# A new order table for an unchanged set of operations: linear attention and a gated MLP on one core

## The chip, the cores and the metric

The kernel runs on one NeuronCore of one Trainium2 chip. The metric is the device time of one execution in microseconds (us). Five engines run in parallel: PE (TensorE, matmuls; PEld is its weight load), DVE (VectorE), ACT (ScalarE), POOL (GpSimd) and SP (SyncE, which issues the DMAs).

## The reference

A gated recurrence over 768 steps for 4 batches of 8 heads with head dimension 48, and behind it an MLP with a spatial gate (d_model 384, d_ff 1024). All inputs are float32.

```python
for t in range(S):                       # q, k, v, alpha: (4, 8, 768, 48)
    state = alpha[:, :, t, :, None] * state + einsum('bhd,bhe->bhde', k[:, :, t], v[:, :, t])
    y[:, :, t] = einsum('bhd,bhde->bhe', q[:, :, t], state)
x = y.transpose(0, 2, 1, 3).reshape(B, S, H * D)
h = maximum(x @ w_in, 0); u, v = h[..., :512], h[..., 512:]
v_n = (v - mean(v)) / sqrt(var(v) + 1e-6)
v_s = einsum('ts,bsd->btd', w_spatial, v_n) + b_spatial[None, :, None]
out = (u * v_s) @ w_out
```

## The kernel before

**Tiling.** The 768 steps of a batch are 6 chunks of 128, so there are 24 chunks. Chunks 0 to 7 are worked in four pairs (`pair`, two steps a partition, loads of 384 KB), chunks 8 to 23 one by one (`first`, loads of 192 KB). Behind a chunk's attention come its parts of the MLP (`second_v`, `second_u`, and per batch `second_s`, `second_o`).

**Names.** Each operation has a key, written here with points. For pair j: `lnp.j` (ACT, logarithm of alpha, L443), `cump.j.par` (PE, cumulative sum with the triangle matrices le_pair and lt_pair, L452), `einvp` and `eexpp` (ACT, two exponentials of it, L460 and L469), `ktp` (POOL or DVE, k times one, L474) and `qtp` (DVE, q times the other, L481), `vbp` (cast of v), `tr.k`/`tr.q` (PE transposes, L502) and `ev.k`/`ev.q` (their copies to SBUF), `sc` (PE scores, L574), `m` (DVE, mask, L585), `updq` (PE, state update), `z` (DVE), `S` and `sb` (POOL: state times decay, state cast), `ya.j` and `y.i` (PE, output inside the pair and from the state), `xs`, `xt`, `xe` (the output cast, transposed, copied to `xT`). `lnp.1` reads the load `ac.2`, since loads are named by the pair's first chunk. Single chunks have the same steps without the p (`ln`, `cum`, `kt`, `trk`, `upd`). Then `v.b.t` and `u.b.f.h` (PE, first MLP matmul and its relu), `bn`, `rs`, `vn` (normalization of v), `s.b.d.h` (PE, spatial matmul on vn, six matmuls in two parts), `g` (gate product), `o.b.t` (last matmul) and `st` (store). Weights are loaded as float32 into two `raw_w` buffers and cast (`cast.w_in.half.n`, `cast.w_sp`, `cast.w_out`); w_spatial is transposed (`wt`, `we`). The constants are `c_*` operations: `c_m2.0` and `c_m2.1` (masks of the pairs), `c_m4`, `c_id` (identity), `c_tri` (le_pair and lt_pair), `c_sbd`, `c_qt`, `c_kt`, `c_la` (memsets). `b_sp` is the load of the spatial bias by POOL's queue, `bb.0` and `bb.1` its spread by PE, `be.0` and `be.1` its copy.

**The order.** Nothing is scheduled at run time. The text `PLAN` is one word an operation: the letter of the engine (P PE, D DVE, A ACT, G POOL, S SP's issue of a DMA, Q its landing, which emits nothing) and the operation's number. `replay` (called at L1129) emits the operations in that order, so each engine, and SP's DMA queue, gets its instructions in the order of its words and works them strictly one after another. A word says too which engine does an operation that several could do (`ENGINES`). Numbers behind a colon are filler: at the next PSUM bank taken, that many columns of a float32 matmul on the tile `junk` (L188), two passes each, go in front.

```python
for word in plan.split():
    number, *junk = word[1:].split(":")
    op, eng = ops[int(number)], LETTERS[word[0]]
    assert eng in op.eng and not op.done and all(d.done for d in op.deps), op.key
    fill.extend(int(x) for x in junk)
    op.emit(eng)
```

The durations given to `Op` (such as 1.46 us for a pair's load, `LP`) were for the planner that wrote the table; at run time they do nothing.

Of the kernel before, what the change touches and what calls it, by code (L numbers as in the profile page):

```python
# [54 lines left out]
LETTERS = {"P": "PE", "D": "DVE", "A": "ACT", "G": "POOL", "S": "SP", "Q": "DMA"}  # L55

PLAN = """
D0 S49 Q50 D17 D13 S109 Q110 G47 Q48 D5 S53 Q54 G10 D7 S51 Q52 D2 D3 D11 G18 D15 D12 D1 S55 Q56 A57 G14 S111 Q112 G16
P58:512:512:192 P264 A59 P68 A60 S113 Q114 G9 A69 D62 A70 D6 P66:512:232 S115 Q116 D71 P262 A67 D4 P74 A117 D61 S178
Q179 D72 A263 P128:492 D75 A265 P118 D73 A129 P76 S19 Q20 P64 A130 G131 D65 A119 D77 S180 Q181 A120 G63 D132  # L60
P134:512:108 P86 G121 D122 A135 P78 D87 S182 Q183 P126 D88 P124 P89 D80 S184 Q185 A186 P136 D91 A79 A127 D90 G81 A137
G123 D83 A125 G82 P149:512:500 A133 S322 Q323 P146 D151 P92 A22 D150 P96 A93 P197 D23 A97 D21 P94 D147 P187 A198 P98
A95 S24 Q25 D148 G200 A188 P100:228 A189 G190 P203 S326 Q327 A199 P138 D191 A101 D201 G84 A99 P195 D102 G8 A204 P205
G85 P193 A139 P103 D140 S324 Q325 A202 D206 G141 D196 P152 A104 D143 G142 A194 P215 S29 Q30 D105 G192 P153 A330 P157
G144 P207 D154 A106 G145 D158 P155 P331 D209 A156 D216 P341 A208 P159 G28 A332 D217 P212 A160 G210 A26 D214 P172 G211
A342 D213 P161 A333 G27 A173 D335 P218 S33 Q34 A343 A162 S328 Q329 P219 D345 P170 G334 A220 S382 Q383 D163 P223 P349
P221 A224 S384 Q385 P164 G344 D350 A222 P339 D174 A171 P225 P337 A165 P168 D340 A226 P166 D107 A175 D338 P227 A167
D176 D108 A169 P230 D32 A228 D177 P238 A231 D31 P247 S386 Q387 D35 A239 P347 D232 A248 P250 P244 A249 P242 G36 D229
A348 P236 A252 D251 P362 A233 S37 Q38 G346 D245 P253 D246 A243 G336 P240 D364 A237 S424 Q425 P351 A390 D363 A255 S428
Q429 D235 P359 A254 D234 P391 A352 D353 S388 Q389 P274 D360 A393 A241 G354 P270 A392 D356 P275 D361 A395 G394 P266  # L70
D276 P267 G357 D396 P271 A40 G39 D268 P398 D272 P259 S426 Q427 G355 A400 P365 D399 A261 D260 P256 G358 P405 S430 Q431
D366 A432 P369 P278 G269 D370 S495 Q496 P367 P433 D258 A368 P371 G273 D257 P279 S41 Q42 D407 A372 P294 A434 G397 D406
P295 A435 S461 Q462 G277 A437 D280 P376 S463 Q464 G436 P408 D296 P282 D438 A409 G439 P401 A377 P290 D402 A503 S465
Q466 P410 P440 G403 D411 P283 D412 A441 G281 D442 P373 D284 G297 P291 A374 P420 D292 S499 Q500 G285 A46 P447 D421 P443
P504 S497 Q498 A469 G43 D378 P413 A45 G404 P470 A44 S592 Q593 D449 P286 A472 A505 D448 P416 S467 Q468 A471 P287 D444
A474 D417 P418 G445 S501 Q502 A507 D288 P306 G473 A414 D508 S594 Q595 A419 P450 D415 G293 A307 P422 A451 S596 Q597
P298 D475 A423 G506 D375 S663 Q664 P477 A299 P452 G476 P302 A479 D453 D478 G289 A600 P480 P510 A303 D481 P484 S626
Q627 G446 D454 A512 P601 D511 P318 D485 G482 A602 S598 Q599 A603 A379 D486 P513 G483 P314 A605 S665 Q666 D515 G604
A319 P487 A509 D606 S628 Q629 P455 A488 D514 P608 S705 Q706 A456 D315 P489 P516 A610 D609 P310 S632 Q633 G607 D490
A517 D457 A491 P615 A671 P518 S630 Q631 P492 D519 A520 D381 A458 P521 D311 A493 D617 P530 A522 S667 Q668 D616 P528  # L80
A494 P611 D380 P534 S707 Q708 A529 D460 A634 P532 D459 D612 A523 S743 Q744 P548 G613 A531 P672 D524 P635 G641 S777
Q778 A713 P540 D533 A535 P618 A525 S709 Q710 P560 A674 A637 A636 D527 P544 D526 S669 Q670 A673 G638 P714 A639 P561
A676 S711 Q712 D640 P549 G614 A619 D677 P541 A715 S779 Q780 G675 D550 A716 P545 A751 D542 P642 S781 Q782 G551 P620
D562 P552 A622 D621 A718 S749 Q750 P553 D546 G543 A643 D719 P645 P623 A644 S745 Q746 D554 G717 A785 D646 P649 A678
P679 S747 Q748 G647 D650 P721 A624 P556 G547 A723 D651 P557 A681 D722 G563 P652 D680 S783 Q784 P682 D558 A653 P686
G555 P728 D683 S877 Q878 P654 D687 P536 A656 G684 A655 P537 D688 A720 S873 Q874 G648 P786 D729 P752 A787 P564 S907
Q908 G685 D538 A754 A758 P724 P657 D730 A753 S875 Q876 G539 A789 P565 D725 A658 D790 S990 Q991 P731 G755 A756 D566
P689 A732 P568 D757 G788 A690 D659 P759 A569 P733 S879 Q880 G726 P691 P576 D734 A692 G559 D625 A735 A760 S909 Q910
P762 P736 A761 G567 D693 D577 S944 Q945 A881 P792 D763 P766 G727 A794 D793 P882 S1027 Q1028 P694 D768 A737 G791 A883
D767 P699 G764 S986 Q987 A884 A695 P795 G765 P769 A886 S950 Q951 D796 P588 A700 G885 A915 D887 S948 Q949 P584 A770  # L90
D797 A696 S946 Q947 P889 D585 P771 A738 P798 D772 P701 A773 D891 A589 D799 P774 A890 D888 S911 Q912 D739 P703 A775
D702 P800 P896 S578 Q579 A704 D801 P580 A660 D802 D898 S304 Q305 P813 A581 D897 S988 Q989 P892 A740 P803 D776 S1023
Q1024 A952 P811 A994 S913 Q914 D661 P697 A814 D742 A804 P916 D741 P572 D893 S300 Q301 A917 D662 A918 P809 D805 G919
A920 S992 Q993 P815 A698 D812 A806 P953 S312 Q313 P829 A955 A573 D808 S590 Q591 P821 D807 A954 S1025 Q1026 D921 P995
A810 P822 G956 A997 S1029 Q1030 A996 P817 A957 D823 G894 S1057 Q1058 P899 A999 P825 D816 G959 A900 P830 D1000 G824
A922 S582 Q583 P818 D958 D831 P826 G998 D819 P901 P923 P960 A903 D827 S1059 Q1060 A925 P837 D902 G828 D820 A962 P926
P838 S1063 Q1064 D961 A924 P904 A1031 D839 S1061 Q1062 G895 P930 D927 A905 P967 S570 Q571 G832 P1002 D931 A1001 P1032
P845 A1004 D968 G928 A1034 P846 A1033 D932 A1003 P833 G1035 D969 A1036 P834 D847 P963 G929 P933 D1037 P853 A934 D964
D835 A1065 G965 P1039 P1009 A854 G1038 P935 D1040 P849 A936 S855 Q856 D1011 G966 A1041 P1005 P1066 A850 P841 D1006
A1067 D1010 S851 Q852 P970 A1069 G1068 P842 A937 D1070 P857 A971 G1007 D843 P972 G1071 P1072 D858 P1046 A973 G1008  # L100
A974 P1012 D1074 A1073 S859 Q860 D1047 P1042 G844 P978 A1013 D1043 P1014 D1048 P1075 A979 G1044 P938 A1015 D1077 G1045
P975 D1076 A939 G836 P1049 A1016 D940 A976 P1078 G840 P1017 A1050 D906 A1079 P982 G848 A1018 D977 P1051 P1080 P980
A1081 A1082 D1053 P861 A983 D1052 D981 P1095 D1019 A862 P1083 A941 A1020 P984 D942 A1084 D1022 P1054 D943 D1085 P1093
A1055 P869 A1096 D1056 A1094 P1089 P865 D1021 A1086 D985 P1097 D1090 A866 P1109 D1087 S867 Q868 P1105 D1088 S308 Q309
P1106 P1091 D1107 P1101 A1092 D870 G1108 P1102 S871 Q872 P1098 D1103 S574 Q575 P1110 D1104 S316 Q317 P1113 D1099 S863
Q864 P1114 S320 Q321 P1121 G1100 D1115 S586 Q587 P1125 D1111 P1122 D1116 G1112 P1126 D1123 P1117 D1127 P1118 D1124
P1128 D1119 P1136 A1129 G1120 P1132 S1130 Q1131 D1137 P1148 S1138 Q1139 A1133 P1144 D1149 S1134 Q1135 P1140 S1150
Q1151 D1145 P1152 S1146 Q1147 A1141 A1153 S1142 Q1143 S1154 Q1155
"""


# [1048 lines left out]
```

## Time and profile before

| | |
|---|---|
| time, median of 3 runs | 142.56 us (142.46 to 143.35) |
| the profiled execution | 142.43 us, its span 140.6 us |
| PE busy | 135.3 us (96%), 1921 matmuls |
| DVE, ACT, POOL busy | 118.5 (84%), 108.1 (77%), 83.9 us (60%) |
| DMA | 28.64 MB, mean 204 GB/s |
| granted clock of TensorE | 0.997 |

The span is the time from the first to the last instruction of the profiled execution; the time around it is the difference of the two numbers. A busy PE contains filler and is counted with modelled ends, so whether it has work without a gap is read from the spacing of its matmuls. DVE, ACT and POOL are idle most at the very start and at the end.

### The profile page before, as it was taken

What the parts mean: (1) busy time and instruction counts of PE and PEld (TensorE: products, weight loads), DVE (VectorE), ACT (ScalarE), POOL (GpSimd) and SP (SyncE); (2) the same over time, 40 slices, a digit from 0 to 9 for tenths busy, and PEclk for the clock granted to TensorE, in tenths of its full rate; (3) what the DMA queues carried; (4) which work ended last, traced back from release to release, by engine and by line L of the source; (5) the groups of instructions that cost most, each with busy time, mean ns of one, the idle gap of its engine ahead of it and who ended that gap; (6) DMA issues with size and microseconds to landing.
All of it is one profiled execution on the core that took longest, in us unless ns stands there. A gap on an engine that the chain in (4) does not pass through costs nothing.

```text
span 140.6 us, 4974 instructions
## 1 busy us (share of the span) xinstructions
PE 135.3 (96%) x1921; PEld 84.1 (60%) x1921; DVE 118.5 (84%) x292; ACT 108.1 (77%) x279; POOL 83.9 (60%) x148
## 2 busy tenths in 40 slices
PE   7999999999999999999999999999999999999990
PEld 3357566574767656665665765656657666566560
DVE  7187799989999789899689999999899899987850
ACT  3487898899976678999989699989967978751021
POOL 6816458861469996970289999402788599002520
PEclk9999999999999999999999999999999999999998
DMA  4999997989999979989999998999999120005535
GB/s 101 320 324 328 338 254 245 295 286 315 267 226 161 306 145 215 203 175 210 188 199 190 188 200 171 199 200 220 257 222 225 71 107 7 0 23 212 215 146 192
DMA packets 89000, 28.64 MB, mean 204 GB/s; under 512 B 83728, under 2 KB 87440, under 8 KB 88976
## 3 DMA queue, kind: packets, MB, share of 16 engines
q1 hardware_dynamic: 88944, 28.32, 81.8%
q8 instruction: 15, 0.25, 0.7%
q14 instruction: 9, 0.07, 0.2%
q0 software_dynamic: 32, 0.00, 0.0%
HBM read 23.60 MB, written 4.72 MB: 201 GB/s over the span
## 4 chain that ended last, share of the span: by engine, by line
PE 59%; ACT 9%; DMA 9%; SPq 7%; POOL 5%; DVE 5%; issue 4%; ACTq 0%; POOLq 0%
PE bank L819 42%; SPq L432 7%; DMA raw_w<-in_moe_w_in_dram 5%; DMA ac<-in_alpha_dram 3%; PE bank L710 3%; PE bank L745 2%; PE bank L773 2%; PE bank L731 2%; PE bank L657 2%; PE bank L767 1%; POOL kt L681 1%; DMA out_dram<-raw_w 1%; PE bank L389 1%; POOL kt L474 1%; ACT vn L880 1%
## 5 line engine op out<-in xcount | busy, mean ns | idle before, releaser
L819 PE MATMUL bank<-w_spT,vn 128*128 128x384 bf16 x192 | 35.9, 326 | 0.0
L980 POOL TENSOR_TENSOR gT<-vsb,uT 128x384 bf16<-128x384 f32 x27 | 25.0, 939 | 12.5 <-DVE vsb L967 12.1
L819 PEld LDWEIGHTS <-vn 128*128 128x128 bf16 x192 | 17.3, 97 | 10.2
L681 POOL TENSOR_TENSOR kt<-kc,binv 128x384 bf16<-128x384 f32 x16 | 14.6, 917 | 11.9 <-ACT bc L676 7.3
L756 DVE TENSOR_TENSOR ptm<-bank,mask 128x512 bf16<-128x512 f32 x32 | 20.5, 680 | 0.7 <-PE bank L745 0.6
L819 PE MATMUL bank<-xT,w_in 128*128 128x384 bf16 x96 | 19.9, 326 | 0.0
L967 DVE TENSOR_TENSOR vsb<-bank,bsp_bc 128x384 f32<-128x384 f32 x31 | 16.6, 551 | 3.6 <-PE bank L819 3.0
L819 PE MATMUL bank<-w_in,xT 128*128 128x512 bf16 x72 | 18.8, 379 | 0.3 <-ACT xT L198 0.2
L819 PE MATMUL bank<-w_out_sb,gT 128*128 128x384 bf16 (+1 forms) x100 | 18.6, 320 | 0.0
L198 ACT COPY kqT<-bank 128x512 bf16<-128x512 bf16 x28 | 15.9, 598 | 2.2 <-PE bank L710 1.5
L335 POOL TENSOR_TENSOR state<-state,bc 128x192 f32<-128x192 f32 x20 | 10.1, 506 | 12.4 <-DVE mvs L896 5.5
L200 POOL CAST sbd<-state 64x192 bf16<-64x192 f32 x40 | 13.7, 341 | 2.1
L204 ACT ACTIVATE v_sb<-bank 128x512 bf16<-128x512 f32 x20 | 12.0, 602 | 2.4 <-PE bank L819 2.3
L884 DVE BATCH_NORM_STATS2 stats<-v_sb 128x6 f32<-128x512 bf16 x20 | 13.6, 682 | 0.0
L204 ACT ACTIVATE uT<-bank 128x384 bf16<-128x384 f32 x23 | 10.9, 492 | 2.2 <-PE bank L819 2.0
L819 PEld LDWEIGHTS <-w_in 128*128 128x128 bf16 x96 | 8.7, 97 | 5.9
L198 ACT COPY xT<-bank 128x192 bf16<-128x192 bf16 (+1 forms) x25 | 9.0, 377 | 4.1 <-PE bank L389 2.9
L819 PEld LDWEIGHTS <-gT 128*128 128x128 bf16 x100 | 8.8, 97 | 5.0
L188 PE MATMUL bank<-junk 128*128 128x512 f32 (+6 forms) x22 | 10.7, 613 | 1.1 <-DVE junk L1050 1.1
L585 DVE TENSOR_TENSOR ptm<-bank,mask 128x512 bf16<-128x512 f32 x16 | 10.3, 682 | 1.0 <-PE bank L574 1.0
L198 ACT CAST x_sb<-bank 128x384 bf16<-128x384 f32 x19 | 9.0, 494 | 2.3 <-PE bank L773 2.3
L916 DVE TENSOR_SCALAR vn<-v_sb,mvs,rstd 128x512 bf16<-128x512 bf16 x24 | 8.9, 404 | 1.5 <-ACT rstd L909 1.5
(129 smaller groups left out, 281.2 us busy)
## 6 DMA issues: line engine op xcount, KB each, us to landing
ac<-in_alpha_dram SPq DMA_DIRECT2D x16, 192.0 KB, 4.0
kc<-in_k_dram SPq DMA_DIRECT2D x16, 192.0 KB, 4.0
qc<-in_q_dram SPq DMA_DIRECT2D x16, 192.0 KB, 4.2
vc<-in_v_dram SPq DMA_DIRECT2D x16, 192.0 KB, 4.0
raw_w<-in_moe_w_spatial_dram SPq DMA_DIRECT2D x3, 768.0 KB, 5.5
out_dram<-raw_w SPq DMA_DIRECT2D x11, 192.0 KB, 2.9
out_dram<-o_sb SPq DMA_DIRECT2D x9, 192.0 KB, 1.9
ac<-in_alpha_dram SPq DMA_DIRECT2D x4, 384.0 KB, 4.6
```

Source lines behind the costliest of these rows:

```text
L188: nc.tensor.matmul(out=flat[:, 0:cols].rearrange("p (a b) -> p a b", a=4), lhsT=junk, rhs=junk[:, None, 0:n].to_broadcast([128, 4, n]), st ...
L198: nc.scalar.copy(out=out, in_=in_)
L200: ENG[eng].tensor_copy(out=out, in_=in_)
L204: nc.scalar.activation(out=out, in_=in_, func=AF.Relu)
L335: ENG[eng].tensor_tensor(out=st["state"], in0=st["state"], in1=st["bc"][:, :, None].to_broadcast([128, HP, D]), op=ALU.mult)
L585: nc.vector.tensor_tensor(out=st[f"ptm{par}"][:, s], in0=st[f"pt{s}{par}"], in1=mask2[:, par], op=ALU.mult)
L681: ENG[eng].tensor_mul(out=k_blocks(kt3)[:, :, :, 0:D], in0=quad(st["kc"]), in1=st["binv"])
L756: nc.vector.tensor_tensor(out=st["ptm"][:, s], in0=st[f"pt{s}"], in1=mask4, op=ALU.mult)
L819: return lambda ps: nc.tensor.matmul(out=out(ps), lhsT=lhsT(), rhs=rhs(), start=start, stop=stop)
L884: nc.vector.bn_stats(out=stats, in_=d["v_sb"][:, tt, :])
L967: nc.vector.tensor_tensor(out=hold["vs"], in0=ps[:, 0:TH], in1=bsp_bc[:, th, :], op=ALU.add)
L980: ENG[eng].tensor_tensor(out=bt[b]["gT"][:, dsl, cols], in0=hold["vs"], in1=bt[b]["uT"][:, dsl, cols], op=ALU.mult)
```

## The change

Only the text `PLAN` is replaced. The operations, their instructions and their data are the same; 300 operations are on PE and 111 DMAs on SP in both tables. What differs:

- **Engines.** 108 operations change engine: 41 from ACT to DVE and 40 from DVE to ACT, 7 from DVE to POOL (among them `ktp.0.0`, `ktp.0.1`) and 6 back, 8 from POOL to ACT and 6 back.
- **Loads.** SP's order was ac.0, ac.2, qc.0, kc.0, vc.0, kc.2, qc.2, vc.2, ac.4, w_in.1, kc.4, qc.4, vc.4, ...; it is ac.0, ac.2, kc.0, qc.0, kc.2, qc.2, vc.0, ac.4, w_in.1, vc.2, qc.4, kc.4, vc.4, .... Later alpha loads move forward: ac.10 from place 31 to 24, ac.18 from 63 to 55, ac.23 from 87 to 68 (counted from 0).
- **Start of POOL.** It was b_sp, c_m4, c_m2.1, c_tri, c_m2.0, c_id, ktp.1.1; it is c_m2.0, b_sp, c_m4, c_id, c_tri, ktp.0.0, c_m2.1, ktp.1.1.
- **Start of PE and ACT.** PE took cump.0.0, bb.1, cump.0.1, tr.q.0.0 first; it takes bb.1, cump.1.0, cump.0.1, cump.0.0, bb.0, cump.1.1, tr.q.0.1. ACT took lnp.0 and four exponentials before lnp.1; it takes lnp.1 and lnp.0 first. `be.0` and `be.1` go from ACT to DVE.
- **Filler.** 4312 columns in six places become 3616 in four: 1216 in front of bb.1, 1140 of tr.q.0.1, 512 of sc.0.0, 748 of ya.0.

The beginnings of the two tables:

```diff
 PLAN = """
-D0 S49 Q50 D17 D13 S109 Q110 G47 Q48 D5 S53 Q54 G10 D7 S51 Q52 D2 D3 D11 G18 D15 D12 D1 S55 Q56 A57 G14 S111 Q112 G16
-P58:512:512:192 P264 A59 P68 A60 S113 Q114 G9 A69 D62 A70 D6 P66:512:232 S115 Q116 D71 P262 A67 D4 P74 A117 D61 S178
-Q179 D72 A263 P128:492 D75 A265 P118 D73 A129 P76 S19 Q20 P64 A130 G131 D65 A119 D77 S180 Q181 A120 G63 D132
...
+D0 S49 Q50 D1 D13 S109 Q110 D15 S51 Q52 D17 G16 D12 S53 Q54 D4 D3 D2 G47 Q48 G10 S111 Q112 G9 S113 Q114 A117 G14 A57
+S55 Q56 P264:512:512:192 P118 D265 P68 D11 P58 S178 Q179 A69 P262 D6 A59 P128 D5 A60 G61 D263 S19 Q20 A70 D62 A119 G18
+D72 A129 S115 Q116 A120 P76:512:512:116 A130 P64 D122 P66 G131 D65 S182 Q183 A73 D77 D67 G71 D132 P86:512 S180 Q181
...
```

In them P58 is cump.0.0, P68 cump.0.1, P118 cump.1.0, P128 cump.1.1, P264 bb.1, P262 bb.0, G47 b_sp, G10 c_m4, G14 c_tri, G16 and G18 c_m2.0 and c_m2.1, G9 c_id, A57 lnp.0, A117 lnp.1, G61 and D61 ktp.0.0.

## What was predicted, before the result was known

> **What bounds the kernel now.** I read the busy time by stretches first, to see where an engine is full. Columns: stretch, its length, then busy us (and instructions) of PE, PEld, DVE, ACT, POOL, the granted clock, DMA share, GB/s.
>
> ```profile
> 0.00:20.00 20.00, 18.95 (x217) 10.47 (x217) 13.48 (x43) 13.98 (x28) 10.57 (x26) 1.00 1.00 278
> 20.00:40.00 20.00, 19.26 (x395) 12.99 (x394) 19.01 (x47) 18.50 (x50) 11.87 (x25) 1.00 0.99 281
> 40.00:120.00 80.00, 79.72 (x1206) 50.30 (x1205) 72.58 (x175) 69.17 (x187) 57.61 (x95) 1.00 0.86 184
> 120.00:140.60 20.60, 17.35 (x109) 10.33 (x107) 13.46 (x30) 6.40 (x18) 3.89 (x4) 0.98 0.37 134
> ```
>
> From 40 us on TensorE is never without work: 79.72 of 80. From 20 to 40 DVE (19.01) and ACT (18.50) are as full as PE. Only the first 20 us have slack, and there the PE time is partly filler (L188, junk).
>
> The chain that ended last says the same in order of time: a DMA queue and the first weight at the start, one row of 93 second-stage matmuls at the end.
>
> ```profile
> 9.02 1.22 SPq L432
> 10.29 6.88 DMA raw_w<-in_moe_w_in_dram
> ...
> 39.45 2.95 PE bank L819 x18
> ...
> 119.20 15.55 PE bank L819 x93
> ```
>
> 93 matmuls in 15.55 us are 167 ns each, a 384-column matmul without a gap. So the time is: when the dense part starts (first vn matmul at 39.3 us), plus 98 us to the last matmul at 137.3, plus an end of 3.3 us (last copy, store, landing) to 140.6. The profiled execution took 142.43, 1.8 more than its span; the median is 142.56.
>
> The start, instruction by instruction:
>
> ```profile
> 1.22 0.67 POOL L1104 DMA_DIRECT2D b_sp_sb<-in_moe_b_spatial_dram  x1 [0.78 <-POOLq L1144]
> 5.27 0.52 PE L452 MATMUL bank<-la,le_pair 128*128 128x384 bf16 x1
> 5.50 1.37 POOL L241 TENSOR_SCALAR_AFFINE_SELECT mask<-mask 64x512 bf16<-64x512 bf16 x2
> 7.18 0.55 DVE L481 TENSOR_TENSOR qt<-qc,bank 128x384 bf16<-128x384 f32 x1 [3.20 <-ACT bank L469]
> 19.51 0.82 PE L819 MATMUL bank<-w_in,xT 128*128 128x512 bf16 x3
> ```
>
> The bias load leaves early, the first cumulative sum runs at 5.27, the first qt product at 7.18 and the first v matmul at 19.51.
>
> **What the change can and cannot move.** The operations are the same; 108 of them change engine and nearly all change place. TensorE's real work is identical. I summed each PE operation's usual spacing: 112.5 us in both orders. In the 98 us of the dense part the irregular waits (over 0.15 us) add to 1.2 us, the largest 0.34 at 75.9 us for a kt of POOL; the rest is work and a regular 0.13 us where one shape follows another. So behind 40 us the new order can win at most 1.2 us and can lose more.
>
> **The supply of instructions** was the planner's aim. The page shows PE's reads as a queue of their own:
>
> ```profile
> q8 instruction: 15, 0.25, 0.7%
> ```
>
> Fifteen packets of 16 KB, 0.9 to 1.8 us each. The first began at 17.35 us with 357 PE instructions done, the second at 20.81 with 481; the trace shows no PE wait that ends with one. I cost this part at 0; what covers it is that a block arrives some 200 instructions early. Without that cover one late read would cost up to 1.8 us. The Trainium skill (Runtime: NRT & Kernel Launch, Instruction fetch mechanics) speaks against the aim too: it says an engine fetches blocks of 256 instructions ahead by itself and that crossing one is mostly hidden; 0.25 MB in 15 packets agrees with the block, and by that rule too the term is 0.
>
> **The start, walked by hand.** Durations are those of the rows; 0.05 to 0.2 us is added from engine to engine as the rows show it. Loads of 384 KB follow each other at 1.2 us (issue rows 1.15 to 1.22 apart), landing from 4.25 on; w_in's 768 KB took 3.2.
>
> 1. POOL now begins with one mask (1.37, cannot start before DVE's memsets, 1.9), then the bias load, mask4 (1.05), ident (0.57) and only then the triangles (1.2): le_pair and lt_pair end at 6.9 instead of 5.55. The bias issues at 3.3 instead of 1.22; its landing took 3.5, so 6.8. PE's first real operation is now the bias matmul, so all four cumulative sums queue behind it, and DVE's copy of the bias (be.1) stands ahead of sbd's, qt's and kt's memsets. First sum 7.1 instead of 5.27. Filler (1216 columns) ends at 5.27 as before; total filler falls from 4312 to 3616 columns, which lies in these waits.
> 2. ACT takes both logarithms first (ac of pair 1 lands at 5.5), so the eight exponentials run in a row from 7.95 to 11.3. Before they ended at 12.5, since lnp.1 stood behind them and the two bias copies were ACT's.
> 3. DVE's first qt product: 9.4 instead of 7.18. Both first kt move from DVE to POOL (0.91 for 0.55), which delays the second one to 13.0.
> 4. scores, masks, ya.0: 17.45 (17.22 before). The 748 filler columns ahead of it (1.3 us) fit the wait for the last mask.
> 5. vc of pair 1 is now behind w_in and lands at 17.2 instead of 12.8, w_in at 16.0 instead of 17.2. x_sb of chunk 0 comes at 18.2 (17.83), the first v matmul at 20.5 (19.51).
> 6. kc of pair 2 is moved behind its qc: 20.2 instead of 18.28. POOL's kt of pair 2 starts at 20.25 (19.22), and the states behind it on POOL give y.2 and y.3 at 24.6 to 24.9 (24.15 and 24.33).
> 7. From there the new order catches up: updq.2 is already done, w_in.0 lands at 26.1 in both, v.0.2 and v.0.3 end at 28.4 in both; the first four u end at 32.7 (32.3).
> 8. First vn matmul: 39.2 (39.3). The matmuls of sc.3.0 (about 0.3) are then still to do.
>
> Start: 39.2 + 0.3 - 39.3 = +0.2 us. Bounds: -0.7 if all PE idle from 20 to 40 (20 - 19.26) vanishes; +2.3 if step 3's lateness is never given back.
>
> **Behind 40 us.** Loads are further ahead: with landing times shifted by the new queue order, no k, q, v or alpha of chunk 10 or later lands less than 4.5 us before PE uses it (before: 3.2, ac of 10). Alpha of chunk 23 goes out 19 places earlier. I find the chains PE to engine to PE no tighter than before: the shortfalls of PE work against their minimum length add to under 0.5 us in both. DVE's share up to y.21 is 2 us larger, inside more than 10 us of slack there. Bounds: -1.2 (all waits gone) and +2.2 (half of the 4.4 us that PE loses beyond its spacing from 20 to 40, the nearest stretch that waits). Nothing excludes either; I take +0.3, near zero because the row says 79.72 of 80.
>
> **End.** Last copy on DVE (0.36) for ACT (0.32), same stores: 0.0, between -0.2 and +0.3.
>
> **Sum:** 0.2 + 0.3 + 0.0 = +0.5. Span 141.1; with 1.8 around it 142.9 against 142.43; on the median 143.1.
>
> **Rivals.**
> (a) Slower: step 3's lateness stays. DVE is 95% busy from 20 to 40; if its small waits stay as long as they were (3.4 us from 7.2 to 39.3), it starts 2.3 us late and its shorter list up to the last vn of batch 0 (27.2 us of work against 28.7, by the rows) gives nothing back, since the two kt that it sheds first go to a POOL that is itself late. Then the dense part starts 2.3 us late: 142.56 + 2.3 = 144.9. It decides from the point where DVE's first qt product comes after 10.5 us, when the landings at 17.2 and 20.2 no longer cover it. For it: DVE and ACT full; against: the waits at loads in steps 5 and 6.
> (b) The clock. Filler passes of 512 columns ran 0.85 us apart until 4.6 us and 0.43 from 7 on; the clock record starts full speed at 6.79. The new order leaves PE idle from 5.3 to 6.8. If full speed comes one such stretch later, ten 384-column matmuls take 0.34 instead of 0.162 (+1.8) and the 1140 filler columns 3.8 instead of 1.9; of these 3.7 about half hides behind steps 5 and 6: +1.9, 144.5. The Trainium skill (TensorE: Matmul & The Clock Gate, Part 1) says that the gate looks at free-running windows of about 3.4 us and opens after a busy one; the trace's 6.79 allows that.
> (c) Faster: start at its low bound (-0.7) and all 1.2 us of dense waits gone: 142.56 - 1.9 = 140.7. For it: earlier loads, 1.4 us less DVE work ahead of the first vn; against: 1.2 is all there is.
> (d) A late instruction read stops PE: +1.8, 144.4. Against: step above.
>
> **Chances.** Forecast 0.46, (a) 0.27, (b) 0.08, (c) 0.15, (d) 0.04. One per cent (1.4 us) is about what a measurement here tells from no change. Faster is (c), 0.15; slower (a), (b), (d), 0.39; same 0.46. The forecast's own range is 142.0 to 144.0. For 8 in 10 I reach to most of (c) and past (a) for start and dense losses together: 141.0 to 145.8.
>
> **What would show it.** First cumulative sum near 7.1 and bias landing near 6.8 (step 1); first qt 9.4; ya.0 17.5; first v matmul 20.5; y.3 near 24.6; first vn matmul near 39.2; PE busy over 79 of 80 from 40 to 120. Wrong if the first vn matmul is off by more than 1.5 us, or if 40 to 120 holds PE waits of over 2 us.

## The result, and the profile after

| | before | after |
|---|---|---|
| time, median of 6 executions each | 142.95 us (142.46 to 144.57) | 144.88 us (143.92 to 146.68) |
| the profiled execution, its span | 142.43, 140.6 us | 144.01, 142.2 us |
| start of the last matmul in the trace | 136.85 us | 138.45 us |

The new order is slower: after to before is 1.0116 [1.0073, 1.016]. In the profiled executions the last matmul starts 1.60 us later, and what follows it is as long as before. The executions differ in the granted clock: in three of the six the mean clock was 0.988 (spans 143.0 to 143.4), in two 1.0 (142.1 and 142.2). Ratios leave out executions over 1.5% above the fastest of the same kernel, here the one with a span of 144.9. The mean clock shows a fall back to half speed but not a late start of full speed: the profiled execution of experiment 3 has a mean of 1.000, although its record of full speed begins only at 13.45 us.

Busy time by stretches of the changed kernel (columns as before the change):

```profile
0.00:20.00 20.00, 17.59 (x249) 10.46 (x250) 13.44 (x43) 12.19 (x25) 13.03 (x30) 1.00 1.01 286
20.00:40.00 20.00, 18.29 (x338) 11.79 (x342) 18.83 (x43) 19.03 (x50) 12.25 (x23) 1.00 0.95 270
40.00:120.00 80.00, 78.30 (x1192) 50.16 (x1200) 73.08 (x176) 65.73 (x180) 56.89 (x92) 1.00 0.85 179
120.00:142.20 22.20, 18.89 (x135) 11.07 (x132) 14.97 (x35) 9.59 (x27) 1.06 (x1) 1.00 0.39 144
```

PE's share fell in both middle stretches, 19.26 to 18.29 and 79.72 to 78.30. Part of this fall is only in the record: the trace of after holds 59 of the 72 matmuls of v (`w_in<-xT`), 36 of 48 between 40 and 120 us, and a missing matmul looks like a hole. Experiment 2 below, which differs in the place of one cast and has a complete trace, shows

```profile
40.00:120.00 80.00, 79.43 (x1216) 50.24 (x1214) 72.85 (x175) 65.96 (x180) 56.76 (x92) 1.00 0.85 180
```

The largest holes of after that are not beside a missing matmul are 0.42 us before 104.66, 0.24 before 91.94 and 0.21 before 83.36. The chain of waits of after, in order of time:

```profile
11.90 7.56 DMA kc<-in_k_dram
19.60 0.93 POOL kt L474
...
32.24 1.11 DVE w_row L200
33.90 1.24 PE bank L819 x5
35.65 1.57 PE bank L819 x9
39.66 3.04 PE bank L819 x18
...
102.88 0.74 issue
104.66 2.11 PE bank L819 x12
...
121.23 16.41 PE bank L819 x98
```

A cast of w_spatial (w_row) now stands in front of the dense part, and the last row of second-stage matmuls starts later. That this chain begins with a load of k and a kt of POOL comes from a gap in the record: the first of the three matmuls of v.0.0 is missing, and the one at 20.56 is the second. Where all three are recorded (experiment 2, whose start is the same), the chain comes from the bias load and the exponentials:

```profile
3.23 3.49 DMA b_sp_sb<-in_moe_b_spatial_dram
...
9.63 0.79 ACT binvp L460 x2
...
18.66 0.49 ACT binvp L460
20.37 0.83 PE bank L819 x3
```

The page's instruction queue is unchanged:

```profile
q8 instruction: 15, 0.25, 0.7%
```

To see where the 1.60 us come from, I took each PE operation's start and compared the two orders at equal PE work done (the sum of the operations' usual spacings, 112.5 us in both). The table gives the delay against the trace of before, for the changed kernel and four experiments explained below; the first column is the time in the trace of before. Which spacing is called usual moves single entries by some tenths; the difference between two columns of the new order in one row, and the last row, are firmer.

| us in before | after | sb.18 early | start of POOL | no meetings | start only |
|---|---|---|---|---|---|
| 5.27 | +1.46 | +1.49 | +0.14 | +1.53 | +1.54 |
| 12.5 | +0.77 | +0.80 | +0.52 | +0.83 | +0.86 |
| 17.4 | +0.09 | +0.13 | -0.15 | +0.17 | +0.19 |
| 31.7 | +0.19 | +0.24 | +1.18 | +0.16 | +0.30 |
| 33.7 | +1.18 | +0.46 | +1.40 | +0.47 | +0.52 |
| 39.5 | +0.44 | -0.31 | +0.56 | +0.10 | +0.05 |
| 44.1 | +0.50 | -0.26 | +0.62 | +0.16 | +1.03 |
| 75.5 | +0.69 | +0.02 | +0.89 | +0.42 | +1.03 |
| 92.8 | +0.55 | -0.22 | +0.67 | +0.19 | +1.03 |
| 97.9 | +0.92 | +0.16 | +1.04 | +0.56 | +1.04 |
| 103.2 | +1.55 | +0.49 | +1.67 | +0.89 | +1.04 |
| 136.7 | +1.60 | +0.53 | +1.72 | +0.95 | +1.03 |

Three things stand in the column of after. The start is 1.46 us late and next to nothing of that is left at 17.4. A step comes at 33.7, partly given back. Another comes between 93 and 103 and stays. The start, from the timeline of the changed kernel:

```profile
3.23 0.67 POOL L1104 DMA_DIRECT2D b_sp_sb<-in_moe_b_spatial_dram  x1
5.32 1.58 ACT L443 ACTIVATE la<-ac 128x768 bf16<-128x768 f32 x2 [3.29 <-DMA ac<-in_alpha_dram]
6.72 0.32 PE L848 MATMUL bank<-b_sp_sb,ones_row 1*128 1x384 bf16 x1 [1.25 <-DMA b_sp_sb<-in_moe_b_spatial_dram]
6.97 0.34 PE L452 MATMUL bank<-la,le_pair 128*128 128x384 bf16 x1
9.25 0.56 DVE L481 TENSOR_TENSOR qt<-qc,bank 128x384 bf16<-128x384 f32 x1
```

The two later steps begin at DVE. Timeline of DVE, then of POOL, in the changed kernel:

```profile
32.16 1.17 DVE L200 CAST w_row<-raw_w 128x768 bf16<-128x768 f32 x1
34.85 1.16 DVE L916 TENSOR_SCALAR vn<-v_sb,mvs,rstd 128x512 bf16<-128x512 bf16 x2
...
102.55 1.14 DVE L200 CAST sbd<-state 64x192 bf16<-64x192 f32 x2
104.06 0.56 DVE L691 TENSOR_TENSOR qt<-qc,bank 128x384 bf16<-128x384 f32 x1
```

```profile
32.04 0.89 POOL L200 CAST w_row<-raw_w 128x768 bf16<-128x768 f32 x1
34.72 0.83 POOL L200 CAST w_row<-raw_w 128x768 bf16<-128x768 f32 x1
...
102.60 1.86 POOL L980 TENSOR_TENSOR gT<-vsb,uT 128x384 bf16<-128x384 f32 x2 [0.28 <-DVE vsb L967]
```

Each DVE row runs beside one of POOL that began just before it or, for the pair of casts of sb.18, just after its first. I call that a meeting. PE waits at the end of both, in the first and the last of these rows (bracket: idle time and what ended it; the row between them is a wait for a kt of POOL):

```profile
33.39 0.35 PE L831 MATMUL bank<-ident,w_row 64*128 64x64 bf16 x12 [0.70 <-DVE w_row L200]
91.94 0.29 PE L710 MATMUL bank<-ident,kt 64*128 64x64 bf16 x8 [0.24 <-POOL kt L681]
104.66 0.65 PE L819 MATMUL bank<-w_spT,vn 128*128 128x384 bf16 x3 [0.42 <-DVE qt L691]
```

### The profile page after: what moved, and what is told of

Read it like the earlier page. It is cut to its first block, busy times and chain, and to the rows that moved or that the text cites. A ratio compares the mean times of both kernels' runs of the same rounds, so it can differ in the third digit from the quotient of the medians.

```text
span 142.2 us, 4928 instructions
## 1 busy us (share of the span) xinstructions
PE 133.1 (94%) x1904; PEld 83.5 (59%) x1917; DVE 120.3 (85%) x294; ACT 106.5 (75%) x280; POOL 83.2 (59%) x145
## 4 chain that ended last, share of the span: by engine, by line
PE 51%; DVE 14%; POOL 8%; SPq 8%; issue 6%; DMA 5%; ACT 5%; DVEq 0%; POOLq 0%
PE bank L819 38%; SPq L432 7%; DMA kc<-in_k_dram 5%; POOL gT L980 3%; DVE stats L884 2%; PE bank L710 2%; POOL kt L681 2%; POOL sbd L200 2%; PE bank L773 1%; DVE vn L916 1%; PE bank L745 1%; DVE ptm L585 1%; PE bank L831 1%; PE bank L389 1%; ACT binv L669 1%
## 5 line engine op out<-in xcount | busy, mean ns | idle before, releaser
L819 PE MATMUL bank<-w_spT,vn 128*128 128x384 bf16 x192 | 35.3, 326 | 0.5 <-DVE qt L691 0.4
L980 POOL TENSOR_TENSOR gT<-vsb,uT 128x384 bf16<-128x384 f32 x25 | 22.8, 923 | 16.5 <-DVE vsb L967 16.4
L819 PEld LDWEIGHTS <-vn 128*128 128x128 bf16 x192 | 17.6, 97 | 11.3 <-issue 0.5
L819 PE MATMUL bank<-xT,w_in 128*128 128x384 bf16 x96 | 19.2, 326 | 0.0
L819 PE MATMUL bank<-w_in,xT 128*128 128x512 bf16 x59 | 16.0, 379 | 1.3 <-issue 0.3
L198 ACT COPY kqT<-bank 128x512 bf16<-128x512 bf16 x22 | 12.4, 592 | 6.0 <-PE bank L710 4.5
L200 POOL CAST sbd<-state 64x192 bf16<-64x192 f32 x36 | 12.3, 341 | 1.9
L198 ACT CAST x_sb<-bank 128x384 bf16<-128x384 f32 x21 | 9.8, 483 | 3.7 <-PE bank L773 2.7
L200 DVE COPY kqT<-bank 128x512 bf16<-128x512 bf16 x26 | 10.1, 414 | 0.5 <-PE bank L502 0.5
L188 PE MATMUL bank<-junk 128*128 128x512 f32 (+3 forms) x18 | 9.2, 647 | 1.1 <-DVE junk L1050 1.1
L916 DVE TENSOR_SCALAR vn<-v_sb,mvs,rstd 128x512 bf16<-128x512 bf16 x24 | 9.5, 431 | 0.7 <-ACT rstd L909 0.7
```

What stands on the lines that cost most here:

```text
L198: nc.scalar.copy(out=out, in_=in_)
L200: ENG[eng].tensor_copy(out=out, in_=in_)
L819: return lambda ps: nc.tensor.matmul(out=out(ps), lhsT=lhsT(), rhs=rhs(), start=start, stop=stop)
L916: nc.vector.tensor_scalar(out=d["vn"][:, t, :], in0=d["v_sb"][:, t, :], scalar1=d["mvs"][:, t, 0:1], scalar2=d["rstd"][:, t:t + 1], op0=AL ...
L980: ENG[eng].tensor_tensor(out=bt[b]["gT"][:, dsl, cols], in0=hold["vs"], in1=bt[b]["uT"][:, dsl, cols], op=ALU.mult)
```

## The experiments

Theory A: the new order puts DVE's casts and copies beside POOL's work, and each such meeting lengthens a DVE instruction that PE is waiting for. Theory B: the loss lies in the order otherwise, in its start or in waits spread over it, as each expectation says. Theory C: the hole in PE's work at 5.3 to 6.8 us upsets the clock.

**1. sb.18 back on POOL** (one word of the new order).

```diff
-P923 D895 G828
+P923 G895 G828
```

> sb.18 goes back from DVE to POOL, at the same place of the table; nothing else. Theory A (DVE and POOL block each other): in the changed kernel sb.18's two casts took 1.14 us on DVE (102.55 to 103.69) beside POOL's gate product, for 0.52 us of sb.1 when POOL was idle; qt.21 and with it the PSUM bank of s.2.0.0 came late, and PE stood 0.58 us. Without it DVE has 1.1 us less ahead of qt.21, the PE wait before s.2.0.0 goes, and the time falls by 0.6 to 0.9 us: ratio to before about 1.005 to 1.008, span about 141.4. Theory B (the late start of the first 10 us is carried to the end): no change, 1.011 to 1.012. Theory C (POOL's place is what counts: sb.18 then delays the gate products by 0.73 us): PE waits for kt.21 or a g instead, time within 0.3 us of the changed kernel.

Ratio 1.0145 [1.0094, 1.0196], no gain. In the trace the step between 98 and 103 us shrank from 0.63 to 0.05, so the wait was this cast's. But that execution lost 1.6 us elsewhere: its delay at 12.5 us was 2.36 instead of 0.77. The stretch from 6.8 to 11 us of this kernel shows why:

```profile
6.80:11.00 4.20, 4.03 (x12) 1.72 (x12) 3.35 (x10) 2.79 (x7) 1.44 (x2) 0.60 1.15 317
```

The granted clock there was 0.60, where before and after have 1.00. The clock record has full speed from 4.25, half speed from 7.66 to 11.07, then full speed again. PE did 12 matmuls where after did 24. What theory C describes is at work in this execution. Its price in the times isn't clear: the four executions with a mean clock of 0.988 or less had spans of 142.7 to 143.2, the two others 142.8 and 144.1.

**2. sb.18 early on DVE** (behind vn.2.4, where POOL is idle).

```diff
-A902 A920 D807 P825
+A902 A920 D807 D895 P825
...
-P923 D895 G828
+P923 G828
```

> sb.18 stays on DVE, but goes ahead of the relu u.2.3.1, at about 100.0 us, where POOL was idle from 95.3 to 100.5. DVE's list has the same length. Theory A: the two casts take about 0.5 us in place of 1.14, so 0.6 us of the 1.1 is gained: time falls by 0.4 to 0.7 us against the changed kernel, ratio about 1.007. If only sb.18's own work on DVE counts and not the meeting with POOL, the casts take 1.1 us there too or the time stays at 1.011. Theory B: 1.011.

Ratio 1.0109 [1.006, 1.0158], where A gave about 1.007 and B 1.011; the profiled execution came at a span of 141.2, 1.0 below after's, the others at 141.7 to 144.5. In that trace both meetings at which PE waited are gone:

```profile
32.02 0.55 DVE L200 CAST w_row<-raw_w 128x768 bf16<-128x768 f32 x1
...
99.23 0.52 DVE L200 CAST sbd<-state 64x192 bf16<-64x192 f32 x2
```

The casts took 0.52 and 0.55 instead of 1.14 and 1.17. For w_row nothing was changed: POOL was at another cast, which had begun 0.16 us ahead of DVE's, while a normalization of DVE still ran, and was itself the one that took longer (1.06 for 0.5). Which one loses changed with a few tenths of a microsecond. The table's column shows both gains: 0.72 at 33.7 and 0.3 behind 98.

**3. The other half of the first meeting: cast.w_sp.0.1 from POOL to ACT.**

```diff
-P230 G32 A245
+P230 A32 A245
```

> The cast of the second piece of w_spatial (cast.w_sp.0.1) goes from POOL to ACT, at the same place; DVE's list is unchanged. In the changed kernel DVE's cast.w_sp.0.0 took 1.17 us (32.16 to 33.33) while POOL worked on cast.w_sp.0.1 (32.04 to 32.92); before it took 0.55. PE stood 0.87 us in front of wt.0. Theory A: cast.w_sp.0.0 takes 0.55 us again and PE starts wt.0 near 32.8 in place of 33.39; the first vn matmul comes 0.2 to 0.5 us earlier (39.1 to 39.4 for 39.59), the end as much, unless ACT's 0.67 us more takes it back: ratio 1.008 to 1.011. If DVE's order alone made the cast late, it stays at 1.17 us and nothing moves. Theory B: nothing at the end.

Ratio 1.0162 [1.0119, 1.0205], a miss. DVE's cast took 0.55 and the step at 33.7 shrank to 0.2, as A wants, but the time did not follow, and sb.18 met POOL again (1.14). In the profiled execution full speed began only at 13.45 us, so its span of 146.4 says nothing on the order. The other five lie at 143.3 and 143.4, three of them with a mean clock of 0.988 and two with 1.0: here the dip left no mark on the span. Whether this kernel is slower than after is not shown, since the intervals overlap.

**4. POOL's start back** (b_sp, c_m4, c_tri first).

```diff
-G16 D12 S53 Q54 D4 D3 D2 G47 Q48 G10 S111 Q112 G9 S113 Q114 A117 G14
+G47 Q48 D12 S53 Q54 D4 D3 D2 G10 G14 S111 Q112 G16 S113 Q114 A117 G9
```

> POOL's first five operations in the order bias load, mask4, triangles, first mask, identity; all else as in the changed kernel. The bias lands near 4.7 and the triangles end near 4.7, so the first cumulative sum runs near 6.0 to 6.3 (when the two logarithms are done) in place of 6.97, and DVE's first qt product near 8.3 to 8.6 in place of 9.25. Theory B (start carried to the end): time falls by 0.7 to 1.0 us, ratio about 1.005. Theory A: the landings of the loads at 16.0, 17.2 and 19.5 us cover it, PE is at the same place by y.3 (24.4) and the end moves by less than 0.2 us: ratio 1.010 to 1.012.

Ratio 1.0109 [1.0067, 1.0151]. PE's first real work comes 1.3 us earlier than in after:

```profile
5.41 0.50 PE L848 MATMUL bank<-b_sp_sb,ones_row 1*128 1x384 bf16 x1
6.29 0.32 PE L452 MATMUL bank<-la,le_pair 128*128 128x384 bf16 x1 [0.39 <-ACT la L443]
...
22.02 0.40 PE L502 MATMUL bank<-ident,kt 128*128 128x128 bf16 x4 [0.58 <-POOL kt L474]
```

At 22 us PE waits for POOL instead, and the delay at the end is 1.72, as in after (1.60). POOL itself had waited 2.38 us for k of pair 2, which landed at 20.92 in place of 19.46. Whether the edit or the execution made that load late is not known, so the trace doesn't show what the early start is worth undisturbed. The times do say that it won nothing, and in after next to nothing of the lateness was left at 17.4: that the start's lateness is kept falls.

**5. After with 768 more filler columns in front of bb.1**, so that PE has no hole.

```diff
-P264:512:512:192
+P264:512:512:192:512:256
```

> The changed kernel with 768 more filler columns ahead of its first bias matmul (1216 become 1984), which fill PE's idle time from 5.3 to 6.9 us; nothing else. So far its runs had spans of 142.1 to 142.2 (three clock records at full speed throughout), 143.0 to 143.4 (mean clock 0.988: one stretch of 3.41 us back at half speed) and 144.9 (full speed only from a later stretch on). Theory C (the hole lets the clock fall back or open late, by where its windows of 3.41 us happen to lie): with the hole filled nearly all runs come at spans of 141.8 to 142.6, the median time is 143.8 to 144.3 against 144.9, mean clock 0.995 or more, full speed from 7.9 us at the latest. If the spread is of another cause, spans of 143.0 to 144.9 stay as frequent as they were. Theory A (DVE and POOL) says that the fast runs do not change: 142.2.

Ratio 1.0135 [1.0087, 1.0183]: no gain in the median, against C as the whole explanation. All six mean clocks are now 0.997 or more, and so are those of the 24 in experiments 7 and 9, which have the same filler (0.988 or less: three of six of after, four of six in experiment 1): the hole makes the dips frequent, but here the spans still spread from 141.8 to 143.8. It is not their only cause: the kernel before, run beside the experiments, dipped in 3 of 84 executions. In the profiled execution sb.1 (0.76 longer) and sb.18 met POOL, and the delay ended at 2.82.

**6. The inverse of 5: before, with a hole** (its first filler 512 columns instead of 1216).

```diff
-P58:512:512:192
+P58:512
```

> The kernel before, with its first filler cut from 1216 to 512 columns, so that PE is idle from about 2.9 to 5.3 us; nothing else. Theory C: full speed comes one stretch later (near 8 to 10.5 us in place of 6.8) or falls back once in many runs; the spans spread like those of the changed kernel, the median is 0.5 to 2 us above the kernel before (ratio 1.004 to 1.014). If filler only takes PE's time, or the spread of the changed kernel has another cause: the same as before within 0.3 us, with as little spread.

Ratio 1.0188 [1.0134, 1.0242], with the order of before untouched. Three executions had a clock of 0.986 to 0.988 and spans of 144.3 to 145.7, three had 0.998 or 0.999 and 142.6 to 143.1, still some 2 us above the 140.6 of before. The stretch from 26 to 32 us of the profiled one:

```profile
26.00:32.00 6.00, 5.48 (x64) 3.12 (x62) 4.32 (x10) 4.10 (x11) 5.18 (x11) 0.72 0.34 108
```

Its clock record opens at 10.55 us (before: 6.79) and falls to half speed once more from 27.61 to 31.03, a stretch of 3.41 us, as long as in experiment 1. A hole at the start is dear by itself.

The Trainium skill (TensorE: Matmul & The Clock Gate, Part 1) says that the gate looks at free-running windows of about 3.4 us, that the same kernel starts up differently from run to run, and that the ramp is under 1% of a typical span. The stretches of 3.41 us and the spread agree. The 1% does not: in experiment 6, ahead of the fall back, ya.0 was at 18.91 us for 17.22, 1.2% of the span, and behind it the delay was 3.54 us at 31.7 us, 2.5%; the measurement decides.

**7. Both mended: 2 and 5 together.**

> The changed kernel with both mended: 768 more filler columns, and sb.18 moved to DVE's place near 100 us as in the run with sb.18 early. Theories A and C together: spans 141.2 to 141.7 in nearly all runs, median time 143.0 to 143.5, ratio to before 1.003 to 1.007. What is left to the kernel before (0.5 us) is new small PE waits of 0.35 to 0.4 us each (s.1.0.1 for a vsb copy, o.1.0 for a gate product, trk.18 for a kt). If the order as a whole is slower by 1.5 us and not these two places, the ratio stays at 1.010 or more.

Ratio 1.008 [1.0047, 1.0113], just above the 1.003 to 1.007 expected, and the lowest so far though its interval overlaps after's; ten of twelve spans lie between 141.3 and 142.6. Experiment 2 is the same kernel without the added filler, and nine of its twelve spans are 143.0 or more, so the hole seems to cost more than the mean clock shows; the ratios, 1.0109 and 1.008, don't separate the two. The trace, of an execution at 144.1, still has three meetings, sb.1 (0.76 longer at 20 us) and vn.0.0 and vn.0.2 (0.51 each).

**8. Before, without three PE waits.** PE's words only:

```diff
-P172 G211 A342 D213 P161 A333
+P161 P172 G211 A342 D213 A333
...
-P250 P244 A249 P242 G36
+P244 A249 P242 P250 G36
...
-P721 A624 P556
+P556 P721 A624
```

> The kernel before with three of its own PE waits taken out by moving one PE word each past its neighbour: wt.2 (waits 0.40 us for a cast) behind wt.0 and u.0.3.1; v.0.2 in front of v.0.3 (which waits 0.4 to 0.5 us for xe.3); s.1.1.1's first part in front of trk.15 (0.34 us for a kt of POOL). If a PE wait anywhere costs its own length at the end, as the comparison of the two traces says, the time falls by 0.7 to 1.1 us: about 141.6, ratio 0.992 to 0.996, faster than both kernels. If DVE or ACT bound the stretch from 20 to 40 us, only the last of the three counts: 0.3 us or less.

Ratio 1.0047 [1.0025, 1.0069]: slower, a miss. In its trace the first two moves only shifted the waits in the stretch where DVE and ACT are full; the delay is 0.56 at 31.7 and 1.10 from 39.5 to the end.

**9. No meetings.** Experiment 7, with sb.1 back on POOL and two casts of w_spatial on DVE as before the change.

```diff
-D85
+G85
...
-D31
+D31 D32
...
-G32
-G35
...
-D176 A228
+D176 D35 A228
```

> The changed kernel with the 768 columns of filler ahead of the bias matmul, sb.18 early on DVE, sb.1 back on POOL, and the casts w_sp.0.1 and w_sp.1.0 on DVE, as in the kernel before. Theory A (the order loses what POOL's instructions take from DVE beside them): every lengthened DVE instruction found so far is gone, the span is that of before within 0.4 us, ratio 1.000 to 1.004. Theory B (each move of one instruction only shifts the waits between the full engines): the two casts (0.55 us each) now lengthen DVE's queue ahead of the vn copies, wt.0 or the first second-stage matmul waits instead, and the ratio stays at 1.006 to 1.010.

Ratio 1.0085 [1.006, 1.011]. In the trace no DVE instruction is lengthened by more than 0.25 us (one cast of POOL is, by 1.07), and full speed begins at 4.97 us; the mean clock is 0.997 or more in every execution, and but for one of 145.0 the spans lie together (141.6 to 142.4). So with A and C out of the way, as far as one trace and the mean clocks can tell, 0.85% is left for B. PE's waits between 40 and 138 us in this kernel (line, waited for: us, times, longest):

```profile
PE bank L710 <- POOL kt L681: 0.2, 1, 0.2
PE bank L819 <- POOL gT L980: 0.2, 1, 0.2
```

The same two stand in after and in experiment 2; before had none of this size there. They are the visible part of it. In spacing rather than idle time, the wait for kt (chunk 18, at 90.7 us) costs 0.40, the one for gT 0.39, one for vsb at 73.4 us 0.35 and one for uT at 100 us 0.21; before's largest was 0.34. Part is made up between them: the column ends at +0.95, of which +0.70 comes between 93 and 103 us.

**10. The inverse of 1: before, with sb.18 on DVE.**

```diff
-Q1062 G895 P930
+Q1062 D895 P930
```

> The kernel before, with sb.18 alone moved from POOL to DVE at the same place of the order. Theory A: it meets POOL's copies there, takes over 1 us for 0.52 and the step of PE's delay behind s.2.0.0 appears as in the changed kernel: +0.5 us, ratio 1.002 to 1.005. Theory B: DVE has its slack there in the old order (72.58 of 80 us busy), the instruction is absorbed, ratio 1.000 within 0.002.

Ratio 1.0037 [1.0004, 1.007], the size that A gave, and the interval just leaves out no change. DVE's timeline:

```profile
107.85 0.77 DVE L200 CAST sbd<-state 64x192 bf16<-64x192 f32 x2
```

It met POOL's gT (106.03 to 108.23) and took 0.77 for 0.52, and the next cumulative sum on PE waited 0.46 us for the state behind it on DVE. The lengthening of 0.25 us is half of what A gave (over 1 us for 0.52), so the rest of the price is the DVE time itself in front of a waiting PE. (This profiled execution had a span of 143.7 where nine of the others had 140.9 to 142.0; place and duration are read, not the span.)

**11. Before, with the last move of experiment 8 alone.**

> The kernel before, with s.1.1.1's matmuls ahead of the transposes of chunk 15, which is where its largest PE wait behind 40 us is (0.34 us at 75.9, for a kt of POOL). If PE alone sets the end there, it is faster by that wait: -0.3 us, ratio 0.998. If the wait only moves to the next copy, ratio 1.000.

Ratio 1.0009 [0.9976, 1.0042]: no measurable change. The delay changes by less than 0.1 us where the wait of 0.34 was; it moved on. No version here beats the kernel before.

**12. A hybrid: the new order's start with the old order's rest.** The first 300 words are those of experiment 7. At its seam the matmuls of s.0.2.0 take the PSUM bank of cum.8 before qt.8 has read it, so its sums differ from the reference's; the instructions are the same in number and shape.

> A hybrid: the first 300 words of the changed kernel's order (all that comes up to the first two vn matmuls, with the 768 columns of filler ahead of the bias matmul), then the rest of the operations in the order and on the engines of the kernel before. If what remains of the loss lies in the first 40 us, the ratio is 1.006 to 1.009, as with the whole new order and the filler. If it lies in the dense part, it is at most 1.003. The seam can cost a wait of its own, 0.2 to 0.4 us, seen in the trace behind 39 us.

Ratio 1.0093 [1.0057, 1.013], which by the number alone says that the loss is in the start. The trace says otherwise. Its delay is 0.05 us at 39.5, and then PE stops inside a row of transposes:

```profile
43.02 0.19 PE L831 MATMUL bank<-ident,w_row 64*128 64x64 bf16 x1
43.82 0.33 PE L831 MATMUL bank<-ident,w_row 64*128 64x64 bf16 x11 [0.61 <-DVE vsb L967]
```

The first of twelve starts at 43.02, the other eleven 0.80 us later. It stands just behind the seam, where the two orders do not fit; I had allowed that 0.4. From 44.1 us to the end the old order adds 0.00 (1.03 to 1.03 over 92 us), where the new one added 0.79 in experiment 9 and 1.10 in after. So in the traces the late start is absorbed and the loss belongs to the new dense order; as a test of the time this run decides nothing, since the seam took what it was to measure.

## Why the prediction was right, and where not

The sign of the shift, most of the start and the end were right; the size was short. 143.1 was forecast and 144.88 measured, 0.9 above the forecast's own range and inside 141.0 to 145.8; the loss, 1.2%, is just past what was called no change. That the wide range holds it is in part luck: it was drawn out to 145.8 for a start that stays late, which did not happen, and what filled it, apart from the clock of rival (b), was lengthened DVE instructions and a slower dense part, which no rival had.

- **Step 1** held: bias landing 6.68 (6.8), first cumulative sum 6.97 (7.1).
- **Steps 2 and 3** held: exponentials 7.83 to 11.14 (7.95 to 11.3), first qt 9.25 (9.4), second kt's end 12.91 (13.0).
- **Step 4** held, 0.4 early: ya.0 at 17.04 (17.45).
- **Step 5** came out right for another reason. The first recorded v matmul is at 20.56, and the one before it, which is missing, started about 20.35 (20.5); the complete traces of experiments 2, 9 and 12 have 20.37, 20.41 and 20.43. The loads came 1.2 us earlier than walked (w_in 14.77 for 16.0) and x_sb at 17.73 (18.2), so the landings did not hold PE. ACT did: its copy to xT ran from 19.79, behind exponentials and a cast of its own.
- **Step 6** held: kc of pair 2 at 19.46 (20.2), y.3 and y.2 at 24.45 and 24.62 (24.6 to 24.9).
- **Step 7** held: v.0.3's end 28.57 (28.4), fourth u's end 32.69 (32.7).
- **Step 8** failed by 0.4: the first vn matmul came at 39.59 for 39.2. Between steps 7 and 8 lies the cast of w_spatial, which took 1.17; in experiment 2, where it took 0.55, the first vn matmul came at 38.84. The start came to +0.44 by the table's row at 39.5, or +0.6 by the prediction's own sum (39.59 + 0.3 - 39.3), against +0.2.
- **Behind 40 us** is the term that was mis-sized: +0.3 was taken and 1.60 less the start, +1.0 to +1.16, came. The bounds of -1.2 and +2.2 hold it. It was put near zero because the row of before said 79.72 of 80; but that row belongs to the old order and says nothing on the slack of the new. In the column of after it comes as +0.11 up to 92.8 us, +0.37 from there to 97.9 (experiments 2 and 9 have the same step), 0.63 to 103.2, where the sb.18 meeting lies, and 0.05 behind it. The sign that was named, PE busy over 79 of 80, fails on the page (78.30), but holds in the complete traces of experiments 2 and 9 (79.43 in both): busy time is too coarse to show a loss of this size. I compared only chains from PE through one engine and back, at their usual durations; instructions that meet on two engines were not in them.
- **End** 0.0, as predicted.
- **Supply of instructions**, costed at 0: 15 reads in both, and no PE wait in either trace ends with one. Rival (d) did not happen.
- **Rival (a)** fell: the first qt was late as said (9.25), below its point of 10.5, and of the 2.3 us feared the first vn matmul was 0.3 late. That landings cover it, as the prediction argued, is not shown: in experiment 2's chain the first v matmul hangs on the bias load and the exponentials. Which wait gave the time back stays open.
- **Rival (b)** named the right hole and was given too little, 0.08; what the mean clocks of after show is a fall back for one stretch, and a late opening they cannot show. In the profiled execution the clock opened at 6.15, earlier than before, so it is not in the 1.60. But three of the five executions that count had a dipped clock and averaged 144.97 against 143.97 for the two others: 1.0 us each, 0.6 in the mean. That is an estimate from five executions, and experiments 1 and 3, where dipped executions were no longer than the rest, speak against reading it as the dip's price.
- **Rival (c)** fell: the dense waits grew.

Together: of the ratio's 1.65 us (0.0116 of about 142.5) up to 0.6 may come with the clock, though filling the hole alone did not lower the median (experiment 5). The rest is put down to the order, which with hole and meetings mended still cost 0.85%, 1.2 us (experiment 9). What remains open is the split inside the order's part: meetings shift by tenths of a microsecond from execution to execution, and experiments 7 and 9, with and without them, are equal (1.008 and 1.0085). Theory A is shown for single waits, not for the total.

## What to carry to other kernels

A busy share of 99.6% describes one order of the work and is no slack for another: walk the new order's short waits too, with durations that allow for what the neighbouring engine does at that moment. A late start is cheap where the work behind it waits for something else, so look for the next wait before you price it. Filler in front of the first matmuls is part of the timing: in experiment 6 PE was some 2 us less busy up to 5.3 us (2.20 for 4.25), and the profiled execution was 3.54 us late by 31.7 us. And count the records before you read a hole or a chain from a trace.

## What the runs showed of the hardware

DVE and POOL lengthen each other's instructions. DVE's 128x768 cast took 1.17 us beside a POOL cast and 0.55 otherwise, the pair of 64x192 casts 1.14 against 0.52, two normalizations 1.16 where two others took 0.70; in experiment 2 it was POOL's 128x384 cast that took 1.06 for 0.5. Which of the two is lengthened changed from one execution to the next.

The Trainium skill (SBUF — State Buffer, Who interferes with whom) says that DVE's copies, casts and tensor-scalar instructions in their fast mode and POOL's instructions take a shared port pair as an exclusive lock for a whole instruction, and that issue order decides who blocks. The rows above agree, except that 0.77 for 0.52 in experiment 10 is a short block, since POOL's row ended during the casts.

The granted clock fell back to half speed for 3.41 us in two profiled executions (experiments 1 and 6), both of kernels that leave PE a hole in its first 7 us, once at 7.66 and once as late as 27.61 us. The stretches between the changes are multiples of the same length (17.07 is five of them). Why one execution falls back and the next does not is open. PE's busy time in the stretch before does not settle it: it was 1.37 and 2.68 of 3.41 us before the two falls, but also 2.31 in experiment 2 (5.66 to 9.07 us) and 2.28 in experiment 4 (19.75 to 23.16 us), and there full speed stayed.
